# An unused 64-byte tile ahead of the working buffers of an attention-plus-GLU kernel

## The chip, the cores and the metric

The kernel runs on one core of a Trainium2 chip. The core has five engines that run side by side and meet through semaphores: TensorE (PE; its weight loads are shown apart as PEld), VectorE (DVE), ScalarE (ACT), GpSimd (POOL) and SyncE (SP), which here only issues transfers. The on-chip memory SBUF has 128 partitions; a tile takes the same range of bytes in each of them. Matmuls read a stationary operand (loaded by a weight load) and a moving operand from SBUF and write to PSUM. The metric is the time of one execution on the device in microseconds. Before the change it was 695.38 us, the median of three runs (695.19 to 695.57).

## The reference

The input x has 2048 tokens of 448 features. It is normalised; the result goes through an attention with a compressive memory (four segments of 512 tokens, 16 heads of 28) and through a gated feed-forward network of width 1792, and both are added to x.

```python
xn = layernorm(x)
return x + A(xn, wq, wk, wv, wo, beta) + B(xn, w_gate, w_up, w_down)

def A(x, ...):                       # for each segment s of 512 tokens
    p = softmax(qs @ ks.T * scale + mask)        # mask: -1e9 where key < query
    a_dot = p @ vs
    a_mem = (phi(qs) @ M) / (phi(qs) @ z + 1e-6)
    o = g * a_mem + (1 - g) * a_dot              # g = sigmoid(beta), per head
    M += phi(ks).T @ vs;  z += phi(ks).sum()     # phi(t) = t + 1 if t > 0 else exp(t)
    return concat(o) @ wo

def B(x, ...):
    return (sigmoid(x @ w_gate) * (x @ w_up)) @ w_down
```

## The kernel before

**Precision by splitting.** Each large matmul operand is split into a high part, rounded to the matmul format, and a low part, the rest (`split`, L84; `transpose_low`, L100). A product is then three matmuls per chunk of the contraction: high by high, high by low, low by high. With 448 = 3 x 128 + 64 features that makes the 11 terms of `TERMS` (L53): three for each full chunk, and two for the last, where high and low share one chunk.

**Stages.** `front` normalises and transposes x into `xs` (four blocks of 512 tokens), computes values (`pv`, L327) and keys with queries (`pp`, L347), stores them to HBM, and keeps the memory M (`pmm`, L375; `n2`, L393). Then the feed-forward network (`gated`, L159) runs over pairs of its 14 slices of width 128 and, for each, over the four blocks: gate and up projections (`pgu`, L241), the activation on ACT and DVE into `hh`, and the down projection (`pd`, L166) added into `acc`. Between its steps the program places steps of the attention: scores (`st`, L604), softmax on ACT, DVE and POOL, and the weighted values (`pa`, L679). `project` (L741) ends with the output projection (`po`, L763), adds it into `acc` and stores the result.

**Order.** The order on PE and on SP is the order in which the program issues it, by hand (`manual_schedule`, L269 and L777). On PE the steps of the feed-forward network and of the projection set the pace; `want` (L782) says how many attention steps have to be out by each of them.

**Where tiles lie.** Pools are laid out in SBUF one behind the other, and inside a pool one tile behind the other, each rounded up to 32 bytes. `keep` comes first: `ident`, the four `xs` (14,336 bytes each), the four `acc` (7,168 each), and the two gates of four numbers each (16 bytes, so 32 bytes each). Behind it lie `mid` (`wgu` and `wo` in buffers of 8 KB, `qk` and `hh` in 4 KB, `sg`, `raw`, `rawd`), `late` (four buffers of 3,584 bytes: `wv` in the front stage, `wdn` in the feed-forward network), and then `front`, whose place `att` takes over later (`qk2`, `w`, `mb`, `vv` and small tiles).

In the program before, `ident` begins at byte 16,512 and `xs` at 17,024, both multiples of 128; `gate` is at 103,040, `gate_n` at 103,072, and the first tile of `mid` at 103,104, which is 64 past a multiple of 128. Since nearly all sizes that follow are multiples of 128, nearly all big tiles behind the gates begin 64 past a multiple of 128. (A few tiles of `front`, `xn` and `e` among them, lie behind small ones and begin at 32 past a multiple of 128.) So the large matmuls have their operands so:

| Line | Result | Stationary operand | Moving operand | Columns | Stationary begins at | Moving begins at |
|---|---|---|---|---|---|---|
| L241 | pgu | wgu | xs | 512 | 64 past 128 | 128 |
| L347 | pp | wqk | xs | 512 | 64 past 128 | 128 |
| L327 | pv | xs | wv | 448 | 128 | 64 past 128 |
| L763 | po | xs | wo | 448 | 128 | 64 past 128 |
| L166 | pd | hh | wdn | 448 | 64 past 128 | 64 past 128 |
| L604 | st | qk2 | qk2 | 128 to 512 | 64 past 128 | 64 past 128 |

The chunks, slices and rows that a matmul takes out of such a tile lie multiples of 256 bytes behind its beginning.

Of the kernel before, what the change touches and what calls it, by code (L numbers as in the profile page):

```python
# [9 lines left out]
F32 = mybir.dt.float32  # L10
# [6 lines left out]
P = 128  # L17
# [44 lines left out]
def kernel(  # L62
# [13 lines left out]
    keep = ctx.enter_context(tc.tile_pool(name="keep", bufs=1))  # L76
# [41 lines left out]

    gate = keep.tile([P, NG], F32, name="gate")
    gate_n = keep.tile([P, NG], F32, name="gate_n")  # L120

    def weigh(pool, num, g, add):

        r = pool.tile([P, 16], F32, name="rc", bufs=2)
        n3 = num.rearrange("p (m c) -> p m c", c=32)
        if add:
            V.tensor_scalar_add(r, n3[:, :, DH], add)
            V.reciprocal(r, r)
        else:
            V.reciprocal(r, n3[:, :, DH])  # L130
        V.scalar_tensor_tensor(n3[:, :, :DH], n3[:, :, :DH], g, r.unsqueeze(2).to_broadcast([P, 16, DH]),
                               op0=ALU.mult, op1=ALU.mult)
# [693 lines left out]
```

## Time and profile before

| What | Value |
|---|---|
| Median of three runs | 695.38 us |
| The profiled execution | 695.5 us |
| Its span (first to last instruction) | 693.8 us |
| HBM read and written | 51.05 and 32.64 MB |
| Transfers issued by SP | 35.9% of 16 engines' span |
| Transfers issued by POOL | 5.2% |

In the rows that follow, a group has its line in the program, the engine, the operation, what it writes and reads, its shape and count; behind the bar its busy time in us, the mean length of one in ns, and the idle time of its engine just before, with what ended it. Matmuls overlap in the pipeline, so the mean length of one is longer than the spacing from one to the next. The chain of waits is followed back from the last instruction, at each step to what released it; in order of time, its pieces give a start, a length and how many instructions of one kind lie in the piece. A row of a stretch gives its bounds, and for PE, PEld, DVE, ACT and POOL the busy time and the count, then the granted PE clock, the share of the DMA engines and GB/s. A DMA queue has its packets, megabytes and share of 16 engines in the stretch asked for.

### The profile page before, as it was taken

Reading aid. Unit: us, or ns where it says so; the run is one execution under the profiler, and the core shown is the slowest. Engines: PE = TensorE matmul, PEld = TensorE weight load, DVE = VectorE, ACT = ScalarE, POOL = GpSimd, SP = SyncE. Lnnn points to the kernel's source line nnn. Section 1 sums busy time; section 2 is a strip of 40 time slices with the busy share of each in tenths; the row PEclk is TensorE's granted clock in tenths of the full one; section 3 lists DMA queues with packets and bytes.
Section 4 is the critical chain, followed back from the end, with each engine's and each line's share of the span. In section 5 each row is a group of like instructions: output and inputs, shape, how many; then the busy total and the mean of one; then the engine's idle time right before and its main releaser. Section 6 shows DMA issues by size and latency. Waiting matters only on the chain.

```text
span 693.8 us, 10446 instructions
## 1 busy us (share of the span) xinstructions
PE 688.1 (99%) x3594; PEld 565.7 (82%) x3594; DVE 570.4 (82%) x994; ACT 344.0 (50%) x563; POOL 147.7 (21%) x349
## 2 busy tenths in 40 slices
PE   8999999999999999999999999999999999999997
PEld 7898878778878787787878878787787878878897
DVE  6765785767889898988898889998889889889863
ACT  5836555343555456544555446455543555446320
POOL 3400020101223122221222223222232322222000
PEclk9999999999999999999999999999999999999999
DMA  7446566696242323233233342324342332333342
GB/s 265 180 147 236 196 220 228 255 326 169 70 99 73 92 86 85 69 118 106 56 71 93 74 127 56 98 56 115 81 113 57 95 71 68 86 87 88 96 149 106
DMA packets 45796, 84.37 MB, mean 122 GB/s; under 512 B 6320, under 2 KB 20400, under 8 KB 45232
## 3 DMA queue, kind: packets, MB, share of 16 engines
q1 hardware_dynamic: 42736, 76.37, 35.9%
q0 software_dynamic: 3008, 7.34, 5.2%
q8 instruction: 28, 0.46, 0.3%
q14 instruction: 24, 0.20, 0.1%
HBM read 51.05 MB, written 32.64 MB: 121 GB/s over the span
## 4 chain that ended last, share of the span: by engine, by line
PE 97%; DMA 1%; DVE 1%; SPq 0%; ACT 0%; issue 0%
PE pgu L241 42%; PE pd L166 20%; PE pp L347 10%; PE st L604 6%; PE pa L679 5%; PE po L763 5%; PE pv L327 4%; PE pmm L375 2%; PE n L393 1%; DMA acc<-in_x 1%; PE pt L95 1%; PE pk L367 1%; DVE stats L286 0%; DVE acc L767 0%; DVE xs L102 0%
## 5 line engine op out<-in xcount | busy, mean ns | idle before, releaser
L241 PE MATMUL pgu<-xs,wgu 128*128 128x512 f32 x1232 | 320.9, 398 | 0.0
L241 PEld LDWEIGHTS pgu<-xs,wgu 128*128 128x128 f32 x1232 | 226.3, 188 | 48.3 <-issue 3.2
L166 PE MATMUL pd<-wdn,hh 128*128 128x448 f32 x672 | 162.3, 368 | 0.0
L166 PEld LDWEIGHTS pd<-wdn,hh 128*128 128x128 f32 x672 | 123.1, 188 | 15.3 <-issue 1.0
L619 POOL TENSOR_SCALAR_AFFINE_SELECT w<-w 128x256 f32<-128x256 f32 (+1 forms) x160 | 81.0, 507 | 255.0 <-ACT w L608 215.0
L659 ACT ACTIVATE w<-w 128x1024 f32<-128x1024 f32 (+1 forms) x96 | 87.1, 915 | 87.5 <-DVE w L658 85.7
L658 DVE TENSOR_TENSOR w<-w,mb 128x1024 f32<-128x1024 f32 (+1 forms) x96 | 99.6, 1048 | 0.2
L608 ACT ACTIVATE w<-st 128x512 f32<-128x512 f32 x128 | 75.0, 588 | 43.4 <-PE st L604 43.3
L621 DVE TRANSPOSE_TENSOR_REDUCE mx<-w 128x32 f32<-128x1024 f32 x64 | 79.0, 1235 | 12.7 <-POOL w L619 12.7
L347 PE MATMUL pp<-xs,wqk 128*128 128x512 f32 x308 | 79.0, 405 | 0.0
L169 DVE TENSOR_TENSOR acc<-pd,acc 128x448 f32<-128x448 f32 x112 | 67.4, 601 | 2.7 <-PE pd L166 2.5
L347 PEld LDWEIGHTS pp<-xs,wqk 128*128 128x128 f32 x308 | 56.8, 188 | 14.5 <-issue 2.4
L604 PE MATMUL st<-qk 84*128 84x128 f32 (+3 forms) x256 | 64.0, 311 | 0.0
L252 ACT ACTIVATE hh<-sg 128x512 fp32r<-128x512 f32 x56 | 35.1, 626 | 43.9 <-DVE sg L250 34.8
L604 PEld LDWEIGHTS st<-qk 84*128 84x128 f32 x256 | 48.3, 189 | 8.9 <-ACT w L608 0.4
L249 ACT ACTIVATE sg<-pgu 128x512 f32<-128x512 f32 x56 | 33.3, 595 | 39.9 <-PE pgu L241 39.9
L648 DVE STREAM_TRANSPOSE mb<-top 128x1024 f32<-128x1024 f32 x32 | 39.8, 1242 | 10.3 <-POOL top L645 10.1
L354 DVE TENSOR_TENSOR qk<-pp,qk 128x512 fp32r<-128x512 f32 x28 | 19.3, 688 | 31.0 <-ACT e L352 24.9
L250 DVE SCALAR_TENSOR_TENSOR sg<-sg,pgu 128x512 f32<-128x512 f32 x56 | 37.4, 667 | 4.7 <-PE pgu L241 4.7
L253 DVE SCALAR_TENSOR_TENSOR hh<-sg,hh 128x512 fp32r<-128x512 f32 x56 | 38.6, 690 | 2.4 <-ACT hh L252 2.2
L327 PE MATMUL pv<-wv,xs 128*128 128x448 f32 x176 | 39.6, 376 | 0.4 <-DVE xs L102 0.3
L679 PE MATMUL pa<-w,vv 128*32 128x128 f32 (+3 forms) x512 | 38.5, 436 | 0.0
(100 smaller groups left out, 638.8 us busy)
## 6 DMA issues: line engine op xcount, KB each, us to landing
qk<-qd SPq DMA_DIRECT2D x192, 112.0 KB
qd<-qk SPq DMA_DIRECT2D x28, 512.0 KB
raw<-in_w_ffn SPq DMA_DIRECT2D x14, 512.0 KB
vd<-vst SPq DMA_DIRECT2D x4, 1024.0 KB
vv<-vd SPq DMA_DIRECT2D x16, 256.0 KB
od<-w POOLq DMA_DIRECT2D x16, 256.0 KB, 4.0
sums<-od SPq DMA_DIRECT2D x32, 128.0 KB
out<-acc SPq DMA_DIRECT2D x16, 224.0 KB
```

What stands on the lines that cost most here:

```text
L166: T.matmul(pd[:, :D], l, r, start=n == 0, stop=n == len(mms) - 1)
L169: V.tensor_add(acc[b][:, t, :], pd[:, :D], acc[b][:, t, :])
L241: T.matmul(dst, wgu[f][:, w, side * P:(side + 1) * P], xs[b][:, a, :], start=n == 0, stop=n == len(TERMS) - 1)
L327: T.matmul(pv[:, :D], xs[b][:, a, t * P:(t + 1) * P], wv[w], start=n == 0, stop=n == len(TERMS) - 1)
L347: T.matmul(pp, wqk[c][:, w, :], xs[b][:, a, :], start=n == 0, stop=n == len(TERMS) - 1)
L604: T.matmul(st[:, at:at + L - kb * P], self.qk[:KS, 1, h, kb * P:(kb + 1) * P], self.qk[:KS, 0, h, kb * P:], start=True, stop=True)
L608: A.activation(w, st, AF.Copy)
L619: G.affine_select(d, d, pattern=pattern, base=0, channel_multiplier=-1, compare_op=ALU.is_ge, fill=MASK)
L621: V.tensor_reduce(mx[:, 16 * (n - 1):16 * (n + 1)], w3[:, n // 2, :2 * L].rearrange("p (b n) -> p b n", n=32), axis=mybir.AxisListType.X, ...
L658: V.tensor_sub(w, w, m)
L659: A.activation(w, w, AF.Exp, scale=SCALE)
L679: T.matmul(pa[32 * j:32 * j + 32, kb * P:], self.vv[:, kb, 32 * j:32 * j + 32], self.pairs[j // 2].block(j % 2, kb), start=kb == 0, stop=k ...
```

## The change

One tile of 16 numbers per partition (64 bytes) is taken from the `keep` pool behind the two gate tiles. Nothing writes or reads it. With it, the first tile of `mid` begins at byte 103,168, a multiple of 128, and all tiles of `mid`, `late`, `front` and `att` lie 64 bytes further on; those that were 64 past a multiple of 128 now begin at one. Operations, their order and their waits are as before.

```diff
     gate = keep.tile([P, NG], F32, name="gate")
     gate_n = keep.tile([P, NG], F32, name="gate_n")
+    keep.tile([P, 16], F32, name="even")
 
     def weigh(pool, num, g, add):
```

## The prediction

> **What bounds the kernel now.** I read the busy shares first, then the chain of waits, then PE's own waits.
>
> ```profile
> span 693.8 us, 10446 instructions
> PE 688.1 (99%) x3594; PEld 565.7 (82%) x3594; DVE 570.4 (82%) x994; ACT 344.0 (50%) x563; POOL 147.7 (21%) x349
> ...
> PE 97%; DMA 1%; DVE 1%; SPq 0%; ACT 0%; issue 0%
> ```
>
> PE is busy nearly throughout, and 97% of the chain that ends last is PE. The next view names what PE stood still for.
>
> ```profile
> engine line waited for: us in total, times, longest us
> PE warm L434 <- POOL ident masks.py:199: 1.5, 1, 1.5
> PE pv L327 <- DVE xs L102: 0.3, 1, 0.3
> PE pt L95 <- DVE xn L312: 0.2, 1, 0.2
> ```
>
> Three waits, 2.0 us together, all of them early, and none on a DMA. After them, the sum of the spacings between matmuls is the time. The groups by line give the counts that I multiply with. (The durations in them overlap, since matmuls are pipelined, so I don't use those.)
>
> ```profile
> L241 PE MATMUL pgu<-xs,wgu 128*128 128x512 f32 x1232 | 320.9, 398 | 0.0
> L166 PE MATMUL pd<-wdn,hh 128*128 128x448 f32 x672 | 162.3, 368 | 0.0
> L347 PE MATMUL pp<-xs,wqk 128*128 128x512 f32 x308 | 79.0, 405 | 0.0
> L763 PE MATMUL po<-wo,xs 128*128 128x448 f32 x176 | 36.5, 363 | 0.0
> L327 PE MATMUL pv<-wv,xs 128*128 128x448 f32 x176 | 39.6, 376 | 0.4 <-DVE xs L102 0.3
> ```
>
> The true spacing stands in the chain of waits in order of time (start, length, what, how many): a piece of PE divided by its count is the time from one matmul to the next.
>
> ```profile
> 115.90 4.41 PE pv L327 x22
> 141.01 2.56 PE pp L347 x11
> 158.21 6.76 PE pgu L241 x29
> ...
> 656.70 1.21 PE pd L166 x6
> 657.91 2.20 PE po L763 x11
> 660.11 1.24 PE pd L166 x6
> ...
> 668.22 22.02 PE po L763 x110
> ```
>
> 512 columns: pgu 6.76/29 = 233.1 ns, pp 2.56/11 = 232.7 ns. 448 columns: po 22.02/110 = 200.2 ns, pv 4.41/22 = 200.5 ns, but pd 1.21/6 = 201.7 and 1.24/6 = 206.7 ns, alternating, mean 204.2. So pd is slower than its two siblings of the same size. The pd and po pieces are neighbours in time, at a granted clock of 0.98 to 1.00 over the tail, so neither the clock nor a busier chip explains it:
>
> ```profile
> 668.00:694.00 26.00, 22.22 (x112) 20.48 (x110) 10.18 (x19) 2.20 (x4) 0.00 (x0) 0.98 0.39 133
> ```
>
> What differs is where the operands lie. pv reads its moving operand from wv, which occupies the very four buffers that wdn of pd takes later. Its stationary operand is xs, whose tiles begin at a multiple of 128 bytes; that of pd is hh, which begins 64 bytes past one.
>
> **The change, part by part.** It adds no instruction, no wait and no DMA, and removes none. It moves ident, xs, acc, gate and gate_n by nothing and every tile behind them by 64 bytes.
>
> (1) The unused tile: nothing writes or reads it. Cost 0.
>
> (2) ACT, DVE and POOL on moved tiles. No row shows a dependence: the copy out of PSUM into the unmoved xs takes as long as that into the moved qk or w.
>
> ```profile
> L97 ACT ACTIVATE xs<-pt 128x512 fp32r<-128x512 f32 x16 | 9.4, 590 | 3.4 <-PE pt L95 3.4
> L348 ACT ACTIVATE qk<-pp 128x512 fp32r<-128x512 f32 x28 | 16.7, 596 | 38.4 <-PE pp L347 36.8 <-DMA phi<-fd 1.5
> L608 ACT ACTIVATE w<-st 128x512 f32<-128x512 f32 x128 | 75.0, 588 | 43.4 <-PE st L604 43.3
> ```
>
> 590, 596 and 588 ns: 1% either way. I take 0. Even 1% of DVE's 570.4 us is 5.7 us on an engine with 123 us to spare, off the chain; PE's work hides it. Without that cover it would cost those 5.7 us.
>
> (3) Transfers into and out of moved tiles. The first stretch is the only one where PE is short of data: its chain holds 7.20 us of waiting for x, behind the loads of wv_raw (moved). Compare a saturated early stretch that fills mostly moved tiles with a late one that only empties acc (unmoved):
>
> ```profile
> 2.67 7.20 DMA acc<-in_x
> ```
> ```profile
> q1 hardware_dynamic: 723, 1.36, 102.9%
> ```
> ```profile
> q1 hardware_dynamic: 432, 0.69, 23.1%
> ```
>
> The first is 8.5 to 12 us: 1.36 MB in 1.029 x 16 x 3.5 = 57.6 engine-us, 23.6 GB/s per engine. The second is 686 to 694 us: 0.69 MB in 0.231 x 16 x 8 = 29.6, 23.3 GB/s. They agree to 1.3%, which of 7.2 us is 0.1 us, either way. I take 0.
>
> (4) The operands of TensorE. Four kinds of placement stand against each other (stationary, moving): pgu and pp (moved, unmoved), po and pv (unmoved, moved), pd and st (moved, moved). No matmul of weight today has both operands on a multiple of 128. The cheapest per column are po and pv (200.2/448 = 0.447 ns), whose stationary tile begins on 128; pgu costs 233.1/512 = 0.455 and pd 204.2/448 = 0.456. So I read the trace as: a stationary tile that begins in the odd half of 128 bytes costs a little on each matmul. The price is the spacing of pd less that of po: 204.2 - 200.2 = 4.0 ns. Its bounds are the two extreme pairs: 201.7 - 200.5 = 1.2 ns and 206.7 - 200.2 = 6.5 ns. I take 4.0, the mean over neighbours in the tail. It falls away on pgu, pp and pd, 1232 + 308 + 672 = 2212 matmuls: 2212 x 4.0 ns = 8.8 us (2.7 to 14.4 us). That pgu and pp pay what pd pays is a guess: no 512-column matmul with an even stationary tile stands in the trace.
>
> [...]
>
> **Sum.** The profiled execution took 695.5 us, 693.8 of span and 1.7 around it; the median of the runs is 695.38, 0.1 us less. Span 693.8 - 8.8 = 685.0, with 1.7 around it 686.7, and 0.1 off for the median: 686.6 us. Its own range is 681.0 (14.4 us) to 692.7 (2.7 us).
>
> The waits behind PE do not take the gain back: PE waits for nobody after the start, DVE's 570.4 us is far below 685, and the loads of raw and qk2 are issued when a buffer comes free, hence earlier too.
>
> **Rivals.**
>
> *No change.* PE doesn't see the address modulo 128, and pd's extra 4 ns comes from how its three-term groups and the short matmuls between them fall into PE's pipeline. For it: pd alternates between 201.7 and 206.7 at one and the same placement, and weight loads last the same for odd and even stationary tiles:
>
> ```profile
> L241 PEld LDWEIGHTS pgu<-xs,wgu 128*128 128x128 f32 x1232 | 226.3, 188 | 48.3 <-issue 3.2 <-DVE qk L354 0.2
> L763 PEld LDWEIGHTS po<-wo,xs 128*128 128x128 f32 x176 | 32.9, 188 | 2.4 <-issue 0.2
> ```
>
> Against it: po and pv, far apart in time, agree to 0.3 ns, and pd lies outside. The time is 695.4 (parts 2 and 3 leave at most some tenths). That the unused tile gets no room at all, so that nothing moves, gives the same time and goes in here. [...]
>
> *Slower: both reads in one half.* What hurts is not an odd stationary tile but the moving and the stationary read of one matmul beginning in the same half of 128 bytes. Today pd (and st) are so, pgu, pp, po and pv are not; the same 4.0 ns of pd over po fits this equally. After the change all operands begin on 128, so the 1232 + 308 + 176 + 176 = 1892 others pay: 1892 x 4.0 ns = 7.6 us, 695.4 + 7.6 = 703.0 us (1.2 ns gives 697.7, 6.5 ns 707.7), while pd stays. From 0.7 ns per matmul (1.4 us) it decides the sign. Against it: it lets pgu cost more per column than po though both read from opposite halves, which the other reading explains.
>
> **How the numbers follow.** About 0.2%, 1.4 us, is what a measurement here can tell from no change. Forecast (faster, all beyond 1.4 us) 0.44; no change 0.28; slower 0.28. I put the forecast ahead since it alone orders pgu, pd, po and pv; not further, since it and the slower rival share their only priced row. The range for all cases: 681.0, the forecast's end, to 703.0, the middle of the slower case, which leaves out about half of 0.28 above and some 0.05 below. Predicted: 686.6 us.
>
> **What would show it.** Right: the pieces of 11 pgu and pp fall from 2.56 to about 2.52 us, pd's six from 1.21 and 1.24 to 1.20, and po and pv stay at 200. Same-half rival: pgu and pp rise to about 2.61 us for 11, po and pv to 204 ns, and pd stays. No change: every spacing stays to a nanosecond. The weight load's 188 ns, ACT's 588 to 596 ns and the instruction counts should hold in any case; if those move, or PE gets waits on DMA, parts (2) and (3) were wrong.

## The result and the profile after

The changed kernel takes 696.15 us (median of 22 runs, 695.99 to 696.72) against 695.46 us before (22 runs): a ratio of 1.001, with a 95% interval of 1.0004 to 1.0017. It is slower by 0.7 us, beyond its interval but within the 0.2% that the prediction set as the bound of no change. The forecast was 686.6 us. In the experiments, three executions were disturbed and took 843 to 1750 us; the ratios leave them out.

The page of the changed kernel, its first lines, the row of SP's transfers and the chain by engine:

```profile
span 694.5 us, 10446 instructions
PE 688.3 (99%) x3594; PEld 566.3 (82%) x3594; DVE 570.5 (82%) x994; ACT 344.2 (50%) x563; POOL 147.8 (21%) x349
...
q1 hardware_dynamic: 42736, 76.37, 34.6%
...
PE 97%; DMA 1%; DVE 1%; SPq 0%; ACT 0%; issue 0%
...
L242 PEld LDWEIGHTS pgu<-xs,wgu 128*128 128x128 f32 x1232 | 226.9, 188 | 47.2 <-issue 3.2
...
L609 ACT ACTIVATE w<-st 128x512 f32<-128x512 f32 x128 | 75.1, 589 | 43.3 <-PE st L605 43.1
```

(All lines of the program are one further on.) The reader is to see that nothing here has moved but the span: the same instructions, the same counts, busy times within 0.6 us of before, weight loads of 188 ns and copies of 589 ns. The share of the transfers has even fallen, from 35.9% to 34.6%. The change shows only in the chain of waits in order of time:

```profile
2.67 7.21 DMA acc<-in_x
...
78.82 4.48 PE pv L328 x22
...
116.13 4.48 PE pv L328 x22
...
131.11 2.55 PE pp L348 x11
...
158.48 6.74 PE pgu L242 x29
```

and in the same view of the tail:

```profile
653.42 1.22 PE pd L167 x6
654.64 2.24 PE po L764 x11
656.88 1.22 PE pd L167 x6
...
668.48 22.45 PE po L764 x110
690.93 0.02 issue
690.95 0.62 DVE acc L768
```

A piece divided by its count is again the spacing. pv went from 4.41 to 4.48 us for 22 and po from 22.02 to 22.45 us for 110: the last stage alone lost 0.43 us. pgu and pp gained a little, 6.76 to 6.74 and 2.56 to 2.55. For all matmuls of a kind, these are the mean spacings from start to start (those over 245 ns, where PE had a gap, are left out) and the sum of all spacings of the kind:

| Kind | Columns | Before, ns | After, ns | Sum before, us | Sum after, us |
|---|---|---|---|---|---|
| pgu | 512 | 233.2 | 232.4 | 292.42 | 291.60 |
| pp | 512 | 233.1 | 232.3 | 74.98 | 74.75 |
| pd | 448 | 202.8 | 203.7 | 138.78 | 139.38 |
| pv | 448 | 200.6 | 203.8 | 38.40 | 39.08 |
| po | 448 | 200.1 | 203.9 | 35.13 | 35.78 |

The losses are 0.60 + 0.68 + 0.65 = 1.93 us and the gains 0.82 + 0.23 = 1.05 us, so 0.9 us more; the first microseconds, where transposes and filler matmuls wait for data, give 0.2 us back. That is the 0.7 us. So the address matters to TensorE, yet neither in the forecast's way nor in that of the slower rival: po and pv, whose stationary tile didn't move, lost most for each matmul; pd, whose two operands moved alike, lost 0.9 ns; and pgu, which should have gained 4.0 ns or lost them, gained 0.8.

### The profile page after: what moved, and what is told of

Same layout as the page of the kernel before. It is cut to its first block, busy times and chain, and to the rows that moved or that the text cites. A ratio compares the mean times of both kernels' runs of the same rounds, so it can differ in the third digit from the quotient of the medians.

```text
span 694.5 us, 10446 instructions
## 1 busy us (share of the span) xinstructions
PE 688.3 (99%) x3594; PEld 566.3 (82%) x3594; DVE 570.5 (82%) x994; ACT 344.2 (50%) x563; POOL 147.8 (21%) x349
## 3 DMA queue, kind: packets, MB, share of 16 engines
q1 hardware_dynamic: 42736, 76.37, 34.6%
## 4 chain that ended last, share of the span: by engine, by line
PE 97%; DMA 1%; DVE 1%; SPq 0%; ACT 0%; issue 0%
PE pgu L242 42%; PE pd L167 20%; PE pp L348 10%; PE st L605 5%; PE pa L680 5%; PE po L764 5%; PE pv L328 5%; PE pmm L376 2%; PE n L394 1%; DMA acc<-in_x 1%; PE pt L95 1%; PE pk L368 1%; DVE stats L287 0%; DVE acc L768 0%; DVE xs L102 0%
## 5 line engine op out<-in xcount | busy, mean ns | idle before, releaser
L253 ACT ACTIVATE hh<-sg 128x512 fp32r<-128x512 f32 x56 | 35.1, 627 | 43.9 <-DVE sg L251 34.6
```

## The experiments

Two theories stood at first, both made from these rows. The relative one: a 448-column matmul costs some 3.7 ns more where its two operands begin in the same half of 128 bytes. The own-half one: an even moving operand costs it, whatever the stationary one does. Each run names what it moves; none changes an instruction that computes. The edits of e1, e2, e4, e9, e11 and e12 are shown against the changed kernel, the others against the kernel before; all ratios are against the kernel before.

### Both operands moved alike: e1_xs_odd

```diff
     make_identity(nc, ident)
+    keep.tile([P, 16], F32, name="even")
     xs = [keep.tile([P, 7, L], F32R, name=f"xs{b}") for b in range(NB)]
...
-    keep.tile([P, 16], F32, name="even")
```

> The unused tile stands ahead of xs, so xs and acc begin 64 past a multiple of 128 and everything behind the gates at a multiple of 128: both operands have changed halves against the kernel before, and each pair lies to one another as before. Relative theory (a 448-column matmul costs about 3.7 ns more where its two operands begin in the same half of 128 bytes): po and pv are back at 200.2 to 200.6 ns (22.02 us for 110 po), pgu and pp at 233.1, and the time is that of before, 695.5 us within 0.3. Own-half theory (an even moving operand costs the 448-column matmuls 3.7 ns, whatever the stationary one does): po and pv stay at 204 ns as in the changed kernel, 352 x 3.7 = 1.3 us, 696.8 us.

It took 695.52 us against 695.51 (ratio 1.0, 0.9991 to 1.0009). Its chain of waits:

```profile
78.62 4.41 PE pv L328 x22
...
158.16 6.76 PE pgu L242 x29
...
668.20 22.02 PE po L764 x110
```

Every operand of the large matmuls has changed its half, and each of these pieces is the one of before, to the last digit. Own halves are out, the forecast's odd stationary tile with them. Since the change moved one operand of po and pv and cost them 3 to 4 ns, what is left is where the two lie to each other.

### The same half, 128 bytes further: e2_pad128

```diff
-    keep.tile([P, 16], F32, name="even")
+    keep.tile([P, 32], F32, name="even")
```

> The unused tile has 128 bytes in place of 64: all later tiles move, but keep their half of 128 bytes. Modulo 128 (both theories): every spacing as before, po 200.2, pd 202.8, pgu 233.2 ns, and the time 695.5 us within 0.3. If the address counts modulo 256 or the size of the shift itself counts, po or pgu differ from before by over 1 ns, that is by over 0.4 us in the time.

It took 693.39 us against 695.51, a ratio of 0.9968 (0.9956 to 0.9981). This was expected of neither theory. The chain of waits:

```profile
78.23 4.45 PE pv L328 x22
...
157.25 6.66 PE pgu L242 x29
...
665.89 22.26 PE po L764 x110
```

6.66/29 = 229.7 ns for pgu, 3.4 ns less than before in this stretch (over all, 230.7 against 233.2), while po rose to 22.26/110 = 202.4. A shift by 128 bytes isn't neutral, so if the difference of the two addresses counts, it does so modulo something larger than 128. (That the size of the shift counts in some other way is still possible here; the sweep below speaks to it.)

### One operand of pd alone: e3_late_even and e4_late_odd

```diff
     late = ctx.enter_context(tc.tile_pool(name="late", bufs=4, reuse_waits="tile"))
+    late.tile([P, 16], F32, name="even_late", bufs=1)
...
+        sb.tile([P, 16], F32, name="odd_front", bufs=1)
         heads = sb.tile([P, P], F32, name="heads", bufs=1)
...
     sb = ctx.enter_context(tc.tile_pool(name="att", bufs=1, reuse_waits="tile"))
+    sb.tile([P, 16], F32, name="odd_att")
```

(e3 on the kernel before; e4 has the tile in `late` alone, on the changed kernel.)

> Against the kernel before, only the pool late (wv, wdn) moves to a multiple of 128. The moving operand of pd is then even beside an odd stationary one, that of pv even beside an even one. Relative theory: pd falls from 202.8 to about 200.3 ns, 672 x 2.5 = 1.7 us, pv rises by 3.3 ns, 176 x 3.3 = 0.6 us: 694.4 us (0.2% faster). Own-half theory: pv rises by 0.6 us and pd doesn't fall: 696.0 us or more.

> The changed kernel with another 64 bytes at the head of the pool late: mid (wgu, wo, hh) even, late (wv, wdn) and front and att odd. Relative theory: pd about 200.3 ns (1.7 us less than before), pv 200.5 as before, po 204 as in the changed kernel (0.65 us more), pgu 232.4 as in the changed kernel (0.8 us less): 693.6 us, 0.25% under the kernel before. Own-half theory: pd as before at 202.8 to 203.7 ns, so about 695.3 us.

e3 took 694.28 us (0.9982, 0.9973 to 0.9991) and e4 694.05 us (0.9979, 0.9971 to 0.9988), near the relative theory's 694.4 and 693.6. pd fell from 202.8 to 201.7 in e3 and to 201.5 in e4, about half of what was expected. In e3 pv rose to 204.5 ns as expected; in e4 it was 202.1, where 200.5 was expected. And pp, of which nothing was expected, fell in both from 233.1 to 229.7 ns: the tiles ahead of `wqk` moved it by 128 bytes, as in e2. That 1.0 us makes up for what pd fell short, so the times agree with the theory better than its steps do.

### The two halves of a sweep: e5_sweep_a and e6_sweep_b

Here d is the start of the stationary operand less that of the moving one, modulo 256. Unused tiles of 32 bytes between the four `xs` give four values of d in one run, since each block of tokens has its own `xs`.

```diff
-    xs = [keep.tile([P, 7, L], F32R, name=f"xs{b}") for b in range(NB)]
+    xs = []
+    for b in range(NB):
+        pad = 0 if b == 0 else 8              # e6: 32 if b == 0
+        if pad:
+            keep.tile([P, pad], F32, name=f"pad{b}")
+        xs.append(keep.tile([P, 7, L], F32R, name=f"xs{b}"))
...
+    keep.tile([P, 40], F32, name="even")      # e6: 8
```

> Unused tiles of 32 bytes between the four xs tiles, and 160 bytes behind the gates so that all later tiles lie as before modulo 256. Let d be the start of the stationary operand less that of the moving one, modulo 256. For xs0 to xs3 pgu and pp have d = 64, 32, 0, 224, and po and pv d = 192, 224, 0, 32. Modulo-256 theory (d alone sets the price): pgu of the block at d = 64 takes 233.1 ns, po at 192 takes 200.2 ns, po at d = 0 takes the 203 ns of pd, and pgu at 224 is nearer to the 229.7 to 230.7 ns of d = 192 than to 233. Modulo-128 theory (the halves, and the shift of 128 bytes had its gain from elsewhere): pgu at d = 64 takes 233.1 as before and differs from d = 0 alone, where it is at 232.4; nothing below 232.

> The other half of the sweep: 128 bytes ahead of xs0, 32 between the xs tiles, later tiles as before modulo 256. For xs0 to xs3 pgu and pp have d = 192, 160, 128, 96, and po and pv d = 64, 96, 128, 160. Modulo-256 theory: pgu at d = 192 takes 229.7 to 230.7 ns and at 128 takes 232.3; po at 64 takes 202.2 and at 128 takes 203.8 ns. Modulo-128 theory: pgu at 192 as at 64, 233.1 ns, and po at 64 as at 192, 200.2 ns.

One execution of each was taken: 695.54 us for e5 and 695.95 us for e6, against 695.27 us. The mean spacings by block, in ns, again without those over 245:

| d of pgu, pp | pgu | pp | d of pv, po | pv | po |
|---|---|---|---|---|---|
| 64 (e5, xs0) | 233.0 | 233.1 | 192 | 201.1 | 200.2 |
| 32 (e5, xs1) | 232.9 | 232.4 | 224 | 206.5 | 206.6 |
| 0 (e5, xs2) | 230.2 | 229.9 | 0 | 202.8 | 206.4 |
| 224 (e5, xs3) | 232.7 | 232.8 | 32 | 204.0 | 204.4 |
| 192 (e6, xs0) | 231.0 | 229.3 | 64 | 201.9 | 201.9 |
| 160 (e6, xs1) | 233.9 | 233.5 | 96 | 200.1 | 200.1 |
| 128 (e6, xs2) | 232.3 | 232.3 | 128 | 204.2 | 204.2 |
| 96 (e6, xs3) | 233.4 | 233.8 | 160 | 205.1 | 205.3 |

In e6 the chain of waits shows the step where xs0 (d = 192 for pp) gives way to xs1 (d = 160), and pv at d = 96 and 128:

```profile
39.93 2.52 PE pp L353 x11
...
44.63 8.81 PE pv L333 x44
...
65.90 2.56 PE pp L353 x11
...
70.21 2.58 PE pp L353 x11
...
78.41 4.49 PE pv L333 x22
```

The modulo-256 theory held in the main: 64 and 192 differ by some 2 to 4 ns in pgu and pp, where modulo 128 had them equal, and the values of the earlier runs come back at their d (pp at 64, 128 and 192: 233.1, 232.3, 229.3; po at 192, 64 and 128: 200.2, 201.9, 204.2). e4's pv, which missed its expectation, lay at d = 64, where pv takes 201.9 here. A shift by 256 bytes is neutral where the sweep has one: in e5 the tiles behind the gates lie 256 bytes further from xs0 than in the kernel before, and pgu, pp, pv and po on xs0 take 233.0, 233.1, 201.1 and 200.2 ns, after 233.2, 233.1, 200.6 and 200.1 over all blocks before. The expectation missed in two points: pgu at d = 224 is at 232.7, not near 230, so the low place at 192 doesn't reach that far; and po at d = 0 is at 206.4, not at 203. Two kinds in different stages, pgu and pp, or pv and po, draw nearly the same curve. The exceptions are po at d = 0, where pv has 202.8, and, smaller, pgu and pp at d = 192 (231.0 and 229.3). The curves of 512 and 448 columns differ: 512 is cheapest at 0 and 192, 448 at 96 and 192.

### All matmuls at a cheap place: e7_all_minus64 and e8_all_and_st

```diff
+    keep.tile([P, 32], F32, name="pad_mid")
...
+    late.tile([P, 16], F32, name="pad_late", bufs=1)
...
-            wo[h] = eight_k(F32R, "wo").rearrange("p c n -> p (c n)")
+            wo[h] = eight_k(F32R, "wo").rearrange("p c n -> p (c n)")[:, 32:]
...
+        sb.tile([P, 32], F32, name="pad_front", bufs=1)
...
+        mid.tile([P, 16], F32, name="pad_4k", bufs=1)
         raw = [four_k(F32, "wv_raw") for _ in range(2)]
...
+    sb.tile([P, 32], F32, name="pad_att")
...
-            self.qk = sb.tile([P, 2, 2, L], F32R, name="qk2", bufs=2)
+            qk = sb.tile([P, 4 * L + 64], F32R, name="qk2", bufs=2)     # e8 alone
+            self.qk = [qk[:, at:at + 2 * L].rearrange("p (h n) -> p h n", h=2) for at in (0, 2 * L + 48)]
...
```

> Unused tiles of 64 or 128 bytes ahead of mid, its 4 KB buffers, late, front and att, and wo read 128 bytes into its buffer, so that pgu, pp, pd, pv and po all have d = 192. Modulo-256 theory: pgu 230.7 ns (2.5 us less than before over 1232), pp 229.7 (1.1 us), pd 201.5 (0.9 us), po and pv as before: 4.5 us less, 691.0 us, and 0.4% below the kernel before. Modulo-128 theory: d = 192 equals d = 64, so pgu and pp stay and only pd gains: 694.6 us.

> As the run before, and in qk2 the keys (stationary in st) lie 192 bytes further from the queries (moving), so that st has d = 192 too. Modulo-256 theory: st of 512 columns falls by 3 ns as pgu does, and the shorter ones by less, 256 matmuls by 1 to 3 ns: 0.3 to 0.8 us less than the run before, 690.4 us. If st doesn't follow, the two runs are equal.

e7 took 692.09 us against 695.27, a ratio of 0.9954 (0.9941 to 0.9967); e8 692.33 (0.9957, 0.9943 to 0.9971). Of the 4.5 us expected of e7, 3.2 came, against 0.9 by modulo 128. Its chain of waits, first over the span and then in the tail:

```profile
78.02 4.41 PE pv L330 x22
89.45 2.54 PE pp L350 x11
...
156.93 6.66 PE pgu L243 x29
```

```profile
649.95 1.20 PE pd L168 x6
651.15 2.20 PE po L768 x11
653.35 1.20 PE pd L168 x6
...
664.75 22.02 PE po L768 x110
```

In the tail pd is now at 1.20/6 = 200.0 ns like po: the gap of 4.0 ns that the prediction priced is closed there. In e3, where `wdn` moved by 64 bytes and `hh`, `xs` and `wo` didn't, the tail has pd at 1.21, so most of the gap went with that distance. The alternation of 1.21 and 1.24 is gone too, but it was gone already in the changed kernel (1.22), at pd's old distance. Over the whole run pd gained less, 202.8 to 202.1.

Of the 1.3 us that are missing in e7, pd accounts for 0.6 (0.27 us less in place of 0.9). The weighted values `pa` took 0.59 us more than before and the scores st 0.20, though their operands kept their distance; in e10 and e11 `pa` took 0.86 and 0.83 us more. No run separates the cause, but the page of e7 shows that PE is no longer alone on the chain that ends last:

```profile
PE 88%; DVE 5%; issue 3%; POOL 1%; DMA 1%; ACT 0%; SPq 0%; POOLq 0%; ACTq 0%
```

It was 97% PE before. The chain leaves PE where a matmul of st waits 0.3 us for ACT, a wait that the kernel before doesn't have. In e8, st took 38.01 us in sum against 38.17 in e7. That doesn't show that st follows d: its sum lay between 37.69 and 38.30 us in traces that left its d as it was. pgu rose from 289.62 to 290.13 at the same d, so nothing was won.

### po alone, in the changed kernel: e9_wo_only and e12_wo_again

```diff
-            wo[h] = eight_k(F32R, "wo").rearrange("p c n -> p (c n)")
+            wo[h] = eight_k(F32R, "wo").rearrange("p c n -> p (c n)")[:, 48:]
```

> The changed kernel, with wo read and written 192 bytes into its buffers: po alone goes from d = 128 to d = 192, nothing else moves. Modulo-256 theory: po falls from 203.9 to about 200.1 ns, 110 po in the tail from 22.45 to 22.02 us, 0.65 us less: 695.5 us, the time of the kernel before. If the loss of the changed kernel has another place, po may fall but the time stays at 696.1.

> The run with wo alone moved, once more, for its trace. Modulo-256 theory: po at 200.1 ns (110 in 22.02 us, 22.45 in the changed kernel); pv still at 203.8, pgu still at 232.4, span 693.8 to 694.0 us. If po's gain is given back elsewhere, po falls and the span stays at 694.5.

e9 took 695.63 us against 695.49 (ratio 1.0001, 0.9992 to 1.001). e12 is the same kernel, executed once for its trace (695.69 us against 695.46). The tail of e12 in its chain of waits:

```profile
656.86 1.23 PE pd L167 x6
658.09 2.21 PE po L764 x11
...
668.39 22.02 PE po L764 x110
```

With d of po back at 192 the 22.45 us are 22.02 again and the span is 694.0 us, against 694.5 in the changed kernel, while pv (203.6) and pgu (232.4) stay as the change left them. So the loss of the last stage is the place of `wo` beside `xs`, and no other work took up what it gave.

### Other low places: e10_zero_and_96 and e11_pad192

e10 has the edits of e7 with other sizes (192 bytes ahead of `mid`, 160 ahead of its 4 KB buffers and of `late`, 192 ahead of `front` and `att`, `wo` 64 bytes in). e11 is the change itself with 192 bytes:

```diff
-    keep.tile([P, 16], F32, name="even")
+    keep.tile([P, 48], F32, name="even")
```

> Other minima of the sweep: pgu and pp at d = 0 (230.0 in the sweep), pd at d = 96 (po took 200.07 there), pv and po at 192. Modulo-256 theory: pgu and pp as in the run with all at 192 within 0.5 ns; pd from 202.1 to about 200.3 ns, 1.2 us: 690.9 us. If what decides is that d = 192 (64 bytes back) fits and the dip of pgu at d = 0 was chance, pgu is at 232 to 233 and the time above 693.

> The change with 192 bytes in place of 64: all later tiles begin at a multiple of 128 again, but pgu, pp, pv and po have d = 0 in place of 128. Modulo-256 theory: pgu and pp 230.0 ns, 1540 x 3.1 = 4.8 us less than before; po 206.4 (1.1 us more) and pv about 203 (0.4 us more): 692.2 us. Modulo-128 theory: as the changed kernel, 696.1 us.

e10 took 692.08 us against 695.49 (0.995, 0.9937 to 0.9963), where 690.9 was expected; e11 took 692.89 us (0.996, 0.9949 to 0.9972), where 692.2 was. d = 0 serves pgu and pp as 192 does: 230.7 and 228.8 ns in e10, 230.0 and 228.9 in e11, so the dip of the sweep was no chance. pd at 96 missed its expectation, with 201.9 ns in place of 200.3. e11's chain of waits:

```profile
115.14 4.46 PE pv L328 x22
156.93 6.60 PE pgu L242 x29
...
665.14 22.30 PE po L764 x110
```

pgu has gained 6.76 - 6.60 = 0.16 us on 29, and po has lost 0.28 us on 110. This run has all its later tiles at multiples of 128, as the change has, and is 3.3 us faster than the change: the multiple of 128 as such does nothing. po took 202.7 ns here at d = 0, like pv, and not the 206.4 of the sweep.

## Why the prediction was wrong

**What held.** Parts (1) to (3) were right: the unused tile, ACT, DVE and the transfers cost or gave nothing on the path. The wait for the first x took 7.21 us after 7.20, and the copies 589 ns after 588. So was the method: PE's spacings alone made the time of this change. (For a gain of the forecast's size the method would not have been enough: with 3 us gained in e7, PE already has a wait for ACT that it didn't have before.)

**The step that failed** is part (4), the reading of the four placements as the price of an odd stationary tile. It forecast 4.0 ns less for pgu, pp and pd and nothing for po and pv. Measured: 0.8 less for pgu and pp, 0.9 more for pd, and 3.2 and 3.7 more for pv and po. e1 refutes the mechanism: all operands changed their half and no mean spacing moved by more than 0.1 ns. What the runs show in its place is that the distance of the two operands modulo 256 goes with most of the variation of the spacing (229.3 to 233.9 ns at 512 columns, 200.1 to 206.6 at 448 in the sweep). The change took pgu and pp from d = 64 to 128, two dear places (233.1, 232.3), and po and pv from 192, one of the two cheapest (200.1 and 200.6), to 128 (204). The price was mis-sized as well: over all 672, pd took 202.8 ns, 2.7 more than po and not 4.0. The guess that a 512-column matmul pays what a 448-column one pays, named as one in the prediction, was wrong as well: the two lengths have different curves.

**The slower rival** had the right kind of cause, a relation of the two operands' places, and for po and pv the right size (4.0 forecast, 3.2 and 3.7 measured). It failed on the halves: at 512 columns d = 0, the same half, is among the cheapest places (230) and d = 64, opposite halves, among the dear ones (233). So pgu and pp, which were to lose 6.2 us, gained 1.05.

**No change** came nearest in its time, for the wrong reason: effects of both signs cancelled to 0.7 us. PE does see the address: e11, a shift by 192 bytes, takes 0.4% off (692.89 us against 695.49).

**A row misread.** pd's alternation between 1.21 and 1.24 us at one placement was put down as a point for the rival of no change, and their mean as a price. The single spacings of the trace show two rhythms at one placement, d = 0: one group of six in the tail runs 207, 207, 206, 207, 207, 206 ns and the next 199, 207, 202, 203, 202, 198. Other kinds at d = 0 have the same two. In e11 po runs like the second (199, 207, 202, 203, 202 and so on), hence its 202.7. In the sweep po at d = 0 follows po at d = 224, which runs at 205 to 208 ns, and stays in that rhythm for nearly all of its 44 matmuls, hence its 206.4; and in e11 itself the last eleven spacings of pv in the first block are at 206 to 209. So at such a place the spacing, 206.4 ns in one run and 202.7 in the other, went with the work before as well. That can also be why pd, with its own operands as before, took 203.7 in place of 202.8 ns in the changed kernel and in e6, but no run shows it. One mean over such a pair can carry a price, but not its cause.

**What stays open.** Why the distance of the two operands counts was not shown: no run separated a matmul from the weight load that runs beside it (PE was busy for 99% of the span, PEld for 82%), nor set apart the work of the other engines, whose tiles moved as well. Nor is it settled why pd gains less over the run (0.7 ns) than in the tail (4 ns), why `pa` and st took longer in the fastest kernels, or what picks one of the two rhythms at d = 0 where no matmul at d = 224 stands ahead.

## What to carry to other kernels

Where a kernel is bound by the spacing of its matmuls, the start of each stationary tile against that of its moving tile is a parameter worth a sweep: here a few unused bytes between pools took 0.5% off (692.1 us against 695.5 in e10), and a single tile of 192 bytes 0.4%. Rounding all tiles up to one alignment is no substitute, since it fixes the distances without choosing them: the change and e11 both have their big tiles at multiples of 128 and took 696.15 and 692.89 us. Before a difference between two groups is put down to one property, list all that differs between them, also relations between operands, and move both operands together as the first experiment.

## What was not expected of the hardware

The spacing of a matmul with 128 stationary columns and operands of four bytes followed d modulo 256 in e5 and e6: from 229.3 to 233.8 ns at 512 columns (pp) and from 200.1 to 206.6 ns at 448 columns (po), in steps of 32 bytes and not smoothly. The length of a weight load in the profile didn't follow it: the mean was 188 ns in the kernel before and in the changed one.

In these traces the time of the transfers went with alignment. SP's queue kept the 16 engines busy for 34.6% of the span in the changed kernel, 34.8% in e12, 35.2% in e1 and 35.3% in e11, where all big tiles behind the gates begin at multiples of 128, and for 35.7 to 36.2% in the kernel before and the other traces that are read, for the same 76.37 MB. With one trace for each kernel, that shows no cause.
